# Attention products on 64x64 tiles, one turn of outputs ahead of the transposes, scores two steps ahead

## Chip, core and metric

The kernel runs on one core of a Trainium2 chip. The metric is the device time of one execution in microseconds (us). Where several executions are timed, their median is given.

## What is computed

Two blocks follow each other: an attention with a decaying state (`lightning_attn`) and a mixer with a two-layer product (`mixer_low_rank`).

```python
B, H, S, D = 4, 8, 768, 64          # q, k, v
block = 64
for b in range(S // block):
    intra = einsum('bhic,bhjc->bhij', qb, kb) * Dmask      # lam ** (i - j) for i >= j, else 0
    intra = einsum('bhij,bhjd->bhid', intra, vb)
    inter = einsum('bhid,bhde->bhie', qb * lam_pow, kv_state)
    out[:, :, sl] = intra + inter
    kv_state = lam_block * kv_state + einsum('bhsd,bhse->bhde', kb_dec, vb)
x = out as (B, S, H * D)
h = x.T @ U @ V                      # rank 32
u = x + h.T
result = u + relu(u @ w_ch1) @ w_ch2 # 512 -> 2048 -> 512
```

All of it is fp32. Everything that the change touches lies in the attention and in the first part of the mixer (`x`, `h`, `u`).

## The kernel before

The tokens are cut into 24 tiles of 128 (six for each of the four batches, `NS = 24`, `NT = 6`), and a tile is one step `s`. The kernel works with blocks of 128 tokens where the reference has 64, which gives the same result with other powers of `lam`. The eight heads form four pairs `a` of two heads `x`.

What a step does, by its names in the code:

- `prep` turns `q` and `k` on TensorE (PE): four transposes into the PSUM tile `pq`, four into `pk`. ScalarE (ACT) copies them to `qt` and `kt`, and the next loads of `q` and `k` are issued on SyncE's queue (SP).
- `scale` and `scale_k` multiply on GpSimd (POOL): `qs` is `qt` with the powers for the state's part of the outputs, `ks` is the raw `k` with those for the state's update.
- `scores` are the products of `kt` and `qt` into two PSUM banks, `pss` (token by token, four pairs, two heads). `masked` multiplies them by the decay mask on VectorE (DVE) into `sm`.
- `inter` is the state's part of the outputs, `qs` by `kv[s]`, into two banks `px`. `intra` adds `sm` by `v` to the same sums, and ACT copies the sum to `x_nat`, the tile of `x`.
- `state` is `ks` by `v` into the bank `pkv`; DVE adds to it the faded old state (`faded`, four small ACT instructions made by `fade`) and stores `kv[s+1]`. The load of the next `v` follows.

From the seventh step on, the mixer's first part runs between these: `low` (the rank-32 product of a whole batch, at the first step of the next batch) and `low_rows`, `mix` (one product, and a DVE addition that makes `u` of a tile that lies seven steps back), `turn` (four transposes of `u`, its store to memory as `u_d`, and the split of its values on DVE), and `turned` (the rest of the split on ACT and POOL). `aside` are pieces of the preparation of the weights, on DVE and, late, on ACT.

The instructions run on each engine in the order in which the code calls them (`manual_schedule`). That order is a list written out by hand, `pieces`, made step by step in the loop that the diff shows. Before the change it is, in a step s: transposes of s+1, `mix`, (`low`), outputs of s, state of s, scores of s+1, the state's part of the outputs of s+1, mask of s+1, `turn`.

PSUM has eight banks here: `pss` two, `px` two, and `pq`, `pk`, `pt` and `pu` one each. All have one buffer, so the next writer waits for the last reader. `pkv` shares the bank of `pk`, `mix` writes to `pu`. In SBUF, `qt`, `kt`, `qs`, `ks` and `kv` have two buffers, `sm` and `faded` one, `x` nine, the raw `q` and `v` three and the raw `k` four.

A product on PE runs on a part of its 128x128 array: the profile writes it as rows*columns, `128*64` for 128 contracted rows and 64 columns of weights. An fp32 product shows as two records.

After the last step the first large products start (`pz`, line 731, and `pd`, line 741), with the last tiles' `mix` and `turn` woven in by hand. They and the second ones (lines 864 to 868) fill TensorE to the end.

Of the kernel before, what the change touches and what calls it, by code (L numbers as in the profile page):

```python
# [8 lines left out]
FP32 = mybir.dt.float32  # L9
# [3 lines left out]
ALU = mybir.AluOpType  # L13

P = 128
# [3 lines left out]
def kernel(  # L19
# [28 lines left out]
    nc = tc.nc  # L48
# [203 lines left out]
    def two_banks(name, tag):  # L252
        return psf.tile([P, 2, N], FP32, tag=tag, name=name)
# [2 lines left out]
        return psf.tile(shape, FP32, tag=tag, name=name)  # L256


    psa = []

    def bank(shape, name, tag):
# [9 lines left out]
    def load(name, s, engine):  # L271
        b, c = divmod(s, NT)
        t = raw_pool.tile(
            [P, H, D], FP32, tag=f"{name}raw", bufs=4 if name == "k" else 3, name=f"{name}raw"
        )
        source = {"q": q, "k": k, "v": v}[name]
        n = H if name == "v" else H // parts(s)
        for h in range(0, H, n):
            engine.dma_start(
                out=t[:, h : h + n, :],  # L280
                in_=source[b, h : h + n, c * P : (c + 1) * P, :].rearrange("h p d -> p h d"),
            )
        raw[s, name] = t
# [50 lines left out]
    xs = {}  # L334
# [25 lines left out]
    def prep(s):  # L360
        for a0 in range(0, HP, HP // parts(s)):
            for name in "qk":
                turn_half(s, a0, name)
        st[s].update(qt=qts.pop(s), kt=kts.pop(s))
        for name in "qk":
            load_next(name)

    def scale_k(s):
        st[s] = {}
        if s % NT < NT - 1:  # L370
            st[s]["ks"] = ks = att.tile([P, HP, 2, D], FP32, tag="ks", bufs=2, name="ks")
            nc.gpsimd.tensor_tensor(
                out=ks,
                in0=raw[s, "k"].rearrange("p (a x) d -> p a x d", x=2),
                in1=rev.rearrange("p x a -> p a x").unsqueeze(3).broadcast_to([P, HP, 2, D]),
                op=ALU.mult,
            )

    def scale(s):

        if s % NT > 0:
            st[s]["qs"] = qs = att.tile([P, HP, P], FP32, tag="qs", bufs=2, name="qs")
            nc.gpsimd.tensor_tensor(out=qs, in0=st[s]["qt"], in1=powq, op=ALU.mult)  # L383
        if s + 1 < NS:
            scale_k(s + 1)

    def fade(s):

        if 0 < s % NT < NT - 1:
# [1 line left out]
            for a in range(HP):  # L391
                nc.scalar.mul(faded[:, a, :], kv[s][:, a, :], lamc[:, a, :])

    def scores(s):
        qt, kt = st[s]["qt"], st[s]["kt"]
        st[s]["pss"] = pss = two_banks("pss", "pss").rearrange("p x (a i) -> p x a i", a=HP)
        for a in range(HP):
            for x in range(2):
                for rows in half if s >= 2 * NT else [slice(0, P)]:
                    nc.tensor.matmul(  # L400
                        out=pss[rows, x, a, :], lhsT=kt[half[x], a, rows],
                        rhs=qt[half[x], a, :], start=True, stop=True,
                    )

    def masked(s):
        pss = st[s].pop("pss")
        st[s]["sm"] = sm = att.tile([P, 2, HP, P], FP32, tag="sm", bufs=1, name="sm")
        for x in range(2):
            nc.vector.tensor_tensor(out=sm[:, x], in0=pss[:, x], in1=mask[:, x], op=ALU.mult)  # L409

    def state(s):
        c = s % NT
        if c < NT - 1:
            ks, vr = st[s]["ks"], raw[s, "v"]
            pkv = one_bank([P, HP, D], "pkv", "pk")
            for a in range(HP):
                for x in range(2):
                    nc.tensor.matmul(  # L418
                        out=pkv[half[x], a, :], lhsT=ks[:, a, x, :], rhs=vr[:, 2 * a + x, :],
                        start=True, stop=True,  # L420
                    )
            kv[s + 1] = att.tile([P, HP, D], FP32, tag="kv", bufs=2, name="kv")
            if c == 0:
                nc.vector.tensor_copy(out=kv[s + 1], in_=pkv)
            else:
                nc.vector.tensor_tensor(out=kv[s + 1], in0=pkv, in1=st[s]["faded"], op=ALU.add)
        del st[s]
        del raw[s, "v"]
        load_next("v")

    def inter(s):

        st[s]["px"] = both = two_banks("px", "px")
        px = both[:, :, 0 : HP * D].rearrange("p x (a e) -> p x a e", a=HP)
        if s % NT == 0:
            return

        for a in range(HP):
            for x in range(2):
                for t in range(2):  # L440
                    nc.tensor.matmul(  # L441
                        out=px[half[t], x, a, :], lhsT=st[s]["qs"][half[x], a, half[t]],
                        rhs=kv[s][half[x], a, :], start=(a == 0), stop=False,
                    )

    def intra(s):
        first = s % NT == 0
        sm, vr, px = st[s]["sm"], raw[s, "v"], st[s]["px"]
        px = px[:, :, 0 : HP * D].rearrange("p x (a e) -> p x a e", a=HP)
        for a in range(HP):  # L450
            for x in range(2):
                for t in range(2):
                    nc.tensor.matmul(  # L453
                        out=px[half[t], x, a, :], lhsT=sm[:, x, a, half[t]],
                        rhs=vr[:, 2 * a + x, :], start=(first and a == 0), stop=(a == HP - 1),
                    )
        xs[s] = x_pool.tile([P, C], FP32, tag="x", name="x_nat")
        nc.scalar.copy(xs[s].rearrange("p (a x e) -> p x a e", a=HP, x=2), px)


    pps = {}

    def low(b):

        tag = "pq" if b else "pu"
        pp = one_bank([P, P], "pp", tag) if b < B - 1 else bank([P, P], "pp", "b2")
        for c in range(NT):
            for g in range(G):
                nc.tensor.matmul(  # L469
                    out=pp[g * R : (g + 1) * R, :], lhsT=u_w[:, c, :],  # L470
                    rhs=xs[b * NT + c][:, g * P : (g + 1) * P],
                    start=(c == 0), stop=(c == NT - 1),
                )
        pps[b] = pp
# [33 lines left out]
    def next_of_low(b):  # L508
        pps[b].pop(0)()

    def mix(s):
        b, c = divmod(s, NT)
        pu = one_bank([P, C], "pu", "pu") if s < NS - NT - 1 else bank([P, C], "pu", "b2")
        nc.tensor.matmul(
            out=pu, lhsT=v_hl[:, c * P : (c + 1) * P], rhs=p_hl, start=True, stop=True
        )
        nc.vector.tensor_tensor(out=xs[s], in0=pu, in1=xs[s], op=ALU.add)

    uhl, ud, turned = {}, {}, {}
    hl_at, d_at = [hl_pool], [d_pool]  # L520
# [37 lines left out]

    pieces = [("prep", 0), ("scale", 0), ("scores", 0), ("inter", 0), ("masked", 0)]
    for s in range(NS):
        b, c = divmod(s, NT)
        done = s - NT - 1
        more = s + 1 < NS
        step = [("prep", s + 1), ("scale", s + 1)] * more + [("fade", s)] * (c == 1)
        step += [("late", s - 1)] * (s == NT)
        step += [("mix", done)] * (0 <= done < NS - NT - 1)
        step += [("low", b - 1)] * (c == 0 and b > 0)
        step += [("low_rows", b - 1)] * (c == 0 and b > 0)  # L570
        step += [("intra", s)]
        step += [("next_of_low", b - 1)] * (c == 0 and b > 0)
        step += [("late", s)] * (s < NT - 1 or s == NT) + [("state", s)]
        step += [("next_of_low", b - 1)] * (c == 0 and b > 0)
        step += [("turned", done - 1)] * (done > 0) + [("late", s)] * (done >= 0)
        step += [("next_of_low", b - 1)] * (c == 0 and b > 0)
        step += [("scores", s + 1)] * more
        step += [("aside", s)] * (s >= 2 * NT)
        step += [("inter", s + 1), ("masked", s + 1)] * more
        step += [("fade", s + 1)] * (more and c > 0)  # L580
        step += [("aside", s)] * (s < 2 * NT)
        step += [("turn", done)] * (done >= 0 and done // TG < FG)
        pieces += step
    waiting = {name: list(range(NS)) for name in "qkv"}

    def load_next(name, engine=nc.sync):
        if waiting[name]:
            load(name, waiting[name].pop(0), engine)
# [1 line left out]

    run = {
        "prep": prep, "fade": fade, "scores": scores, "masked": masked, "inter": inter,
        "intra": intra, "state": state,
        "low": low, "low_rows": low_rows, "next_of_low": next_of_low, "mix": mix, "turn": turn,
        "scale": scale, "turned": lambda s: turned.pop(s)(),
    }
# [71 lines left out]
    nc.scalar.dma_start(out=lam_row[:, 0:H], in_=lam.unsqueeze(0))  # L668
    load_next("q", nc.sync)
    load_next("k", nc.scalar)  # L670
    for name in "qkvkv":
        load_next(name)
    aside(-1)
    for name in "qkv":
        load_next(name)
    make_identity(nc, ident)
    keep_busy(2)
    pl = one_bank([P, H], "pl", "pt")
# [3 lines left out]
    constants()  # L682
    powers()
    nc.vector.tensor_copy(out=rev, in_=mask[:, :, :, P - 1])
    scale_k(0)
    run.update(aside=aside, late=on_scalar_late)
    for what, s in pieces:
        run[what](s)
# [278 lines left out]
```

## Time and profile before

| | us |
|---|---|
| median of three runs | 673.26 (672.52 to 673.44) |
| the profiled execution | 672.44 |
| its span, first to last instruction | 670.6 |
| TensorE busy in it | 664.3 |
| DVE, ACT and POOL busy in it | 497.5, 277.8 and 112.1 |
| first `px` product, first `pz` product | 8.87 and 119.65 |

The granted TensorE clock was 1.0 all through. The attention stage, from the start to about 119 us, is less than a fifth of the span and holds nearly all of POOL's work. A busy engine in the profile is one that has an instruction in it: matmuls overlap, and their ends are modelled, so starts are the better measure on PE. A bracket at the end of a line of the timeline tells how long the engine had been idle before it, and what ended that.

### The profile page before, as it was taken

To read this page: it belongs to the slowest core of one execution; us is meant where nothing else is said; L and a number is where in the kernel's file an instruction comes from. 1 tells how busy PE (TensorE), PEld (TensorE's weight loads), DVE (VectorE), ACT (ScalarE), POOL (GpSimd) and SP (SyncE) were. 2 spreads that over 40 slices of the span, in tenths; PEclk is the share of its full clock that TensorE was granted. 3 is DMA by queue.
4 is the path that set the end of the run, shared out by engine and by line. 5 is a ranking of instruction groups with operands and counts; after the bars stand their busy time and mean duration, and the time that the engine had idled before them with its cause. 6 is when DMAs were issued, how large, how long until landed. Compare 5 with 4: busy or idle time off the path is not lost.

```text
span 670.6 us, 13171 instructions
## 1 busy us (share of the span) xinstructions
PE 664.3 (99%) x5124; PEld 544.3 (81%) x5124; DVE 497.5 (74%) x873; ACT 277.8 (41%) x517; POOL 112.1 (17%) x92
## 2 busy tenths in 40 slices
PE   9999999999999999999999999999999999999997
PEld 7988989788888888888888888888888888888885
DVE  5688999877999777777797256787586775865864
ACT  4675867554555444444454121332322322322320
POOL 4555757330000000000000000030030300300300
PEclk9999999999999999999999999999999999999999
DMA  9999993254776555555577999854363352443421
GB/s 208 220 217 244 238 243 114 89 197 157 257 260 235 205 203 205 204 204 205 203 282 270 314 321 394 285 182 132 94 218 96 116 199 94 162 152 95 165 86 63
DMA packets 131775, 131.27 MB, mean 196 GB/s; under 512 B 81346, under 2 KB 89794, under 8 KB 131714
## 3 DMA queue, kind: packets, MB, share of 16 engines
q1 hardware_dynamic: 130656, 130.18, 60.8%
q8 instruction: 40, 0.66, 0.4%
q10 hardware_dynamic: 1058, 0.26, 0.2%
q14 instruction: 21, 0.17, 0.1%
HBM read 80.09 MB, written 50.33 MB: 194 GB/s over the span
## 4 chain that ended last, share of the span: by engine, by line
PE 95%; DVE 2%; DMA 1%; ACT 1%; issue 0%; ACTq 0%; SPq 0%; DVEq 0%
PE pz L731 27%; PE pz L866 13%; PE pd L741 13%; PE pz L864 13%; PE pd L868 13%; PE px L453 3%; PE pss L400 3%; PE put L531 1%; PE pkv L418 1%; PE pq L355 1%; PE px L441 1%; PE pk L355 1%; PE pp L469 1%; DVE sm L409 1%; DMA u_d<-x_nat 1%; DMA kraw<-in_k_dram 1%
## 5 line engine op out<-in xcount | busy, mean ns | idle before, releaser
L731 PE MATMUL pz<-u_hl,w 128*128 128x512 f32 x768 | 190.5, 398 | 0.0
L731 PEld LDWEIGHTS pz<-u_hl,w 128*128 128x128 f32 x768 | 144.1, 189 | 35.3 <-issue 0.4
L866 PE MATMUL pz<-w_hl,m 128*128 128x512 f32 x384 | 151.2, 397 | 0.0
L864 PE MATMUL pz<-w_hl,m 128*128 128x512 f32 x384 | 151.0, 397 | 0.0
L868 PE MATMUL pd<-w_d,m 128*128 128x512 f32 x384 | 149.6, 397 | 0.0
L847 ACT ACTIVATE m<-mt 128x512 fp32r<-128x512 f32 x96 | 60.6, 632 | 196.9 <-PE pd L868 142.3
L848 DVE SCALAR_TENSOR_TENSOR m<-rm,m 128x512 fp32r<-128x512 f32 x96 | 71.4, 746 | 54.5 <-ACT m L847 54.3
L893 POOL TENSOR_TENSOR o<-o,u 128x512 f32<-128x512 f32 x20 | 29.8, 1520 | 447.4 <-DVE o L889 447.4
L746 DVE SCALAR_TENSOR_TENSOR r<-pd,r 128x512 f32<-128x512 f32 x96 | 61.8, 686 | 53.2 <-ACT r L737 38.8
L741 PE MATMUL pd<-u_d,w 128*128 128x512 f32 x384 | 98.6, 397 | 0.0
L737 ACT ACTIVATE r<-pz 128x512 f32<-128x512 f32 x96 | 52.2, 596 | 93.0 <-PE pz L731 92.9
L866 PEld LDWEIGHTS pz<-w_hl,m 128*128 128x128 f32 x384 | 72.4, 189 | 17.6
L864 PEld LDWEIGHTS pz<-w_hl,m 128*128 128x128 f32 x384 | 72.4, 188 | 17.6
L868 PEld LDWEIGHTS pd<-w_d,m 128*128 128x128 f32 x384 | 72.4, 189 | 17.5
L741 PEld LDWEIGHTS pd<-u_d,w 128*128 128x128 f32 x384 | 72.2, 189 | 17.2
L849 DVE SCALAR_TENSOR_TENSOR m<-m 128x512 fp32r<-128x512 f32 x96 | 69.1, 721 | 0.9
L846 DVE TENSOR_SCALAR mt<-rm 128x512 uint32<-128x512 uint32 x96 | 46.1, 481 | 26.5 <-DMA rm<-r_d 26.2
L409 DVE TENSOR_TENSOR sm<-pss,mask 128x512 f32<-128x512 f32 x48 | 30.9, 684 | 6.8 <-PE pss L400 6.6
L212 ACT CAST w<-wt 128x512 fp32r<-128x512 f32 x32 | 19.9, 621 | 30.6 <-DVE wt L209 23.4
L453 PEld LDWEIGHTS px<-vraw,sm 128*64 128x64 f32 x768 | 24.6, 138 | 5.9 <-DVE sm L409 2.3
L383 POOL TENSOR_TENSOR qs<-qt,powq 128x512 f32<-128x512 f32 x20 | 25.9, 1296 | 20.7 <-ACT qt L358 20.7
L453 PE MATMUL px<-vraw,sm 128*64 128x64 f32 x768 | 28.2, 226 | 0.4 <-DVE sm L409 0.3
(88 smaller groups left out, 680.4 us busy)
## 6 DMA issues: line engine op xcount, KB each, us to landing
r_d<-r SPq DMA_DIRECT2D x96, 256.0 KB, 2.6
rm<-r_d SPq DMA_DIRECT2D x96, 256.0 KB, 2.7
words<-in_moe_w_ch_dram SPq DMA_DIRECT2D x30, 512.0 KB, 4.3
w_d<-w SPq DMA_DIRECT2D x16, 768.0 KB, 3.3
w_hl<-w_d SPq DMA_DIRECT2D x16, 512.0 KB, 6.0
vraw<-in_v_dram SPq DMA_DIRECT2D x24, 256.0 KB, 4.8
u_d<-x_nat SPq DMA_DIRECT2D x24, 256.0 KB, 3.6
u<-u_d SPq DMA_DIRECT2D x24, 256.0 KB, 3.9
```

The lines of the kernel that those rows point to most:

```text
L453: nc.tensor.matmul(out=px[half[t], x, a, :], lhsT=sm[:, x, a, half[t]], rhs=vr[:, 2 * a + x, :], start=(first and a == 0), stop=(a == HP - 1),
L731: nc.tensor.matmul(out=acc[g][0], lhsT=w[:, n, ct, :], rhs=uhl[g][:, n, ct, :], start=(ct == 0 and n == 0), stop=(ct == CT - 1 and n == 1),)
L737: nc.scalar.mul(rs[g], acc[g][0], 4096.0 + 1.0)
L741: nc.tensor.matmul(out=acc[g][1], lhsT=w[:, 2, ct, :], rhs=ud[g][:, ct, :], start=(ct == 0), stop=(ct == CT - 1),)
L746: nc.vector.scalar_tensor_tensor(rs[g], acc[g][1], 4096.0, rs[g], ALU.mult, ALU.add)
L846: nc.vector.tensor_scalar(t.bitcast(U32), r.bitcast(U32), HI, None, ALU.bitwise_and)
L847: nc.scalar.activation(out=m[:, 0], in_=t, func=AF.Relu)
L848: nc.vector.scalar_tensor_tensor(m[:, 1], r, 0.0, hi, ALU.max, ALU.subtract)
L849: nc.vector.scalar_tensor_tensor(m[:, 2], hi, E, low, ALU.mult, ALU.subtract)
L864: nc.tensor.matmul(out=pz, lhsT=m[:, 0, cols], rhs=hl[:, 0], start=first, stop=False)
L866: nc.tensor.matmul(out=pz, lhsT=m[:, 1, cols], rhs=hl[:, 1], start=False, stop=end)
L868: nc.tensor.matmul(out=pd, lhsT=m[:, 2, cols], rhs=dd, start=first, stop=end)
```

## The change

- Outputs and state are made in two turns, each of products of 64 tokens (`outputs(s, turn)`). The part of an output that the mask makes zero (late keys, early queries) is left out. In a turn, heads of one parity take the first half of the keys and the others the second, so that two row halves of the array never write one bank together. Turn 0 (`ahead`) stands at the end of step s-1, before the next transposes; turn 1 in `intra`. The last two steps use full columns (`whole`).
- The state's products share the two banks of `px` (`pkv` is a part of it), and `state` is merged into `intra`: the copy to `x_nat` comes first, then `kv`.
- Transposes and scores are made two steps ahead instead of one: a short step -1 is put in front. `pss` becomes one fixed tile, `sm` gets two buffers, the raw `k` three instead of four, with its load in a piece of its own after `scale`.
- `scores` use 64x64 tiles in every step (before, from step 12), and from the second tile on leave out the masked quarter. In steps 0 to 6, where there is no `mix`, the first pair's scores (`some_scores`) stand before `intra` and the others after.
- `fade` stands after `prep`, `turn` at the next step after the transposes, and `mix` is parted: its product stays (now in the bank of `pq`), its addition `mixed` comes after `intra`. `low` of the first three batches uses `pu`.

```diff
@@ load @@
-            [P, H, D], FP32, tag=f"{name}raw", bufs=4 if name == "k" else 3, name=f"{name}raw"
+            [P, H, D], FP32, tag=f"{name}raw", bufs=3, name=f"{name}raw"
...
@@ scale @@
+        scale_k(s)
         if s % NT > 0:
...
-        if s + 1 < NS:
-            scale_k(s + 1)
...
@@ scores @@
+    def scores(s, pairs=range(HP)):
         qt, kt = st[s]["qt"], st[s]["kt"]
-        for a in range(HP):
+        for a in pairs:
             for x in range(2):
-                for rows in half if s >= 2 * NT else [slice(0, P)]:
+                for rows in half:
+                    cols = slice(rows.start if s else 0, P)
                     nc.tensor.matmul(
-                        out=pss[rows, x, a, :], lhsT=kt[half[x], a, rows],
-                        rhs=qt[half[x], a, :], start=True, stop=True,
+                        out=pss[rows, x, a, cols], lhsT=kt[half[x], a, rows],
+                        rhs=qt[half[x], a, cols], start=True, stop=True,
                     )
+    def some_scores(s):
+        scores(s, range(1))
+
+    def other_scores(s):
+        scores(s, range(1, HP))
...
@@ inter @@
+        both = two_banks("px", "px")
+        st[s]["px"] = px = both[:, :, 0 : HP * D].rearrange("p x (a e) -> p x a e", a=HP)
+        st[s]["pkv"] = both[:, :, HP * D : (HP + 2) * D].rearrange("p g (a e) -> p g a e", a=2)
...
+    def outputs(s, turn):
...
+        for a in range(HP):
+            for r in range(2):
+                x = r ^ turn
+                for t in range(r, 2):
+                    nc.tensor.matmul(
+                        out=px[half[t], x, a, :], lhsT=sm[half[r], x, a, half[t]],
+                        rhs=vr[half[r], 2 * a + x, :], start=(x, t) not in begun,
+                        stop=last and a == HP - 1 and (turn == 1 or (x, t) == (0, 0)),
+                    )
+                    begun.add((x, t))
+        if last:
+            return
+        ks = st[s]["ks"]
+        for n in range(2):
+            for r in range(2):
+                side = r ^ turn
+                a = 2 * side + n
+                for x in range(2):
+                    nc.tensor.matmul(
+                        out=pkv[half[x], side, n, :], lhsT=ks[half[r], a, x, :],
+                        rhs=vr[half[r], 2 * a + x, :], start=(side, x) not in begun,
+                        stop=(turn == 1 and n == 1),
+                    )
+                    begun.add((side, x))
...
+    def ahead(s):
+        if s < NS - 2:
+            outputs(s, 0)
+
+    def intra(s):
+        if s < NS - 2:
+            outputs(s, 1)
+        else:
+            whole(s)
         xs[s] = x_pool.tile([P, C], FP32, tag="x", name="x_nat")
-        nc.scalar.copy(xs[s].rearrange("p (a x e) -> p x a e", a=HP, x=2), px)
+        nc.scalar.copy(xs[s].rearrange("p (a x e) -> p x a e", a=HP, x=2), st[s]["px"])
+        if s % NT < NT - 1:
+            kv[s + 1] = att.tile([P, HP, D], FP32, tag="kv", bufs=2, name="kv")
+            to, pkv = kv[s + 1].rearrange("p (g a) d -> p g a d", g=2), st[s]["pkv"]
...
+                nc.vector.tensor_tensor(out=to, in0=pkv, in1=faded, op=ALU.add)
+        del st[s]
+        del raw[s, "v"]
+        load_next("v")
...
@@ mix @@
-        pu = one_bank([P, C], "pu", "pu") if s < NS - NT - 1 else bank([P, C], "pu", "b2")
+        pu = one_bank([P, C], "pu", "pq") if s < NS - NT - 1 else bank([P, C], "pu", "b2")
...
@@ the order @@
-    pieces = [("prep", 0), ("scale", 0), ("scores", 0), ("inter", 0), ("masked", 0)]
-    for s in range(NS):
+    pieces = [("prep", 0), ("scale", 0), ("scores", 0), ("masked", 0)]
+    for s in range(-1, NS):
...
-        step = [("prep", s + 1), ("scale", s + 1)] * more + [("fade", s)] * (c == 1)
+        step = [("prep", s + 2), ("scale", s + 2), ("load_k", s)] * more
+        step += [("fade", s)] * (s >= 0)
         step += [("late", s - 1)] * (s == NT)
-        step += [("mix", done)] * (0 <= done < NS - NT - 1)
-        step += [("low", b - 1)] * (c == 0 and b > 0)
-        step += [("low_rows", b - 1)] * (c == 0 and b > 0)
-        step += [("intra", s)]
...
-        step += [("late", s)] * (s < NT - 1 or s == NT) + [("state", s)]
+        step += [("turn", done - 1)] * (done > 0 and (done - 1) // TG < FG)
+        mixes = 0 <= done < NS - NT - 1
+        step += [("mix", done)] * mixes
+        step += [("low", b - 1), ("low_rows", b - 1)] * batch
+        apart = s >= 0 and more and not mixes
+        step += [("some_scores", s + 2)] * apart
+        step += [("intra", s)] * (s >= 0)
+        step += [("mixed", done)] * mixes
...
-        step += [("scores", s + 1)] * more
-        step += [("aside", s)] * (s >= 2 * NT)
-        step += [("inter", s + 1), ("masked", s + 1)] * more
-        step += [("fade", s + 1)] * (more and c > 0)
-        step += [("aside", s)] * (s < 2 * NT)
-        step += [("turn", done)] * (done >= 0 and done // TG < FG)
+        if s < 0:
+            step += [("inter", 0), ("ahead", 0), ("scores", 1), ("masked", 1)]
+        else:
+            step += [("other_scores" if apart else "scores", s + 2)] * more
+            step += [("aside", s)] * (s >= 2 * NT)
+            step += [("inter", s + 1), ("ahead", s + 1)] * next_
+            step += [("masked", s + 2)] * more
+            step += [("aside", s)] * (s < 2 * NT)
```

## The prediction

> **What bounds the kernel now.** I read the page first, then busy time by stage, then the waits and the timeline of the attention stage.
>
> ```profile
> PE   9999999999999999999999999999999999999997
> PE 95%; DVE 2%; DMA 1%; ACT 1%; issue 0%; ACTq 0%; SPq 0%; DVEq 0%
> ...
> 7.00:28.00 21.00, 20.90 (x490) 18.72 (x486) 11.01 (x25) 13.02 (x34) 11.55 (x10) 1.00 0.99 226
> 66.00:95.75 29.75, 29.41 (x756) 26.55 (x754) 28.34 (x50) 20.65 (x46) 20.16 (x16) 1.00 0.96 238
> ```
>
> The first two lines are the page's PE row of 40 slices and the chain that ended last: TensorE from end to end. The last two are stretches (length, busy PE, weight loads, DVE, ACT, POOL, clock, DMA share, GB/s). Even with DMA 99% busy, PE has no holes, and in the second stretch DVE is nearly full too (28.34 of 29.75). All that changes lies before 119.65 us, where the last `px` product gives way to `pz`; what follows is one unbroken PE stream, so time won or lost here moves the end by as much. The waits of that stage give PE almost none: 2.3 us over nine times on `sm`, 0.7 on `x_nat`, 0.3 on `kt`.
>
> Why there are none is seen in one early step, then in a step with the mixer's pieces (start, duration, engine, what):
>
> ```profile
> 16.74 0.66 PE L355 MATMUL pq<-ident,qraw 128*128 128x128 f32 x4
> ...
> 17.49 0.59 ACT L358 COPY qt<-pq 128x512 f32<-128x512 f32 x1 [0.70 <-PE pq L355]
> ...
> 17.76 1.15 PE L453 MATMUL px<-vraw,sm 128*64 128x64 f32 x32
> ...
> 17.97 0.59 ACT L358 COPY kt<-pk 128x512 f32<-128x512 f32 x1
> ...
> 18.75 0.64 PE L418 MATMUL pkv<-vraw,ks 128*64 128x64 f32 x16
> 18.96 0.59 ACT L458 COPY x_nat<-px 128x512 f32<-128x512 f32 x1 [0.40 <-PE px L453]
> ...
> 19.31 1.16 PE L400 MATMUL pss<-qt,kt 64*128 64x128 f32 x16
> ...
> 19.50 0.42 DVE L426 TENSOR_TENSOR kv<-pkv,faded 128x256 f32<-128x256 f32 x1 [1.25 <-PE pkv L418]
> ...
> 20.40 0.72 PE L441 MATMUL px<-kv,qs 64*64 64x64 f32 x32
> ...
> 21.05 0.66 PE L355 MATMUL pq<-ident,qraw 128*128 128x128 f32 x4
> ```
>
> ```profile
> 100.41 1.15 PE L453 MATMUL px<-vraw,sm 128*64 128x64 f32 x32
> ...
> 101.01 1.07 ACT L392 ACTIVATE faded<-kv,powq 128x64 f32<-128x64 f32 x4
> ...
> 101.40 0.64 PE L418 MATMUL pkv<-vraw,ks 128*64 128x64 f32 x16
> ...
> 101.96 1.10 PE L400 MATMUL pss<-qt,kt 64*64 64x128 f32 x32
> ...
> 102.89 0.64 PE L441 MATMUL px<-kv,qs 64*64 64x64 f32 x32
> ...
> 103.46 0.66 PE L531 MATMUL put<-ident,x_nat 128*128 128x128 f32 x4
> ```
>
> The copy of `kt` (until 18.56) lies beside `px`. `x_nat` (until 19.55) lies beside `pkv` and `pss`. `kv` (until 19.92) lies beside `pss`, and the product that needs it starts at 20.40, 0.48 later. An early step is 4.31 us (16.74 to 21.05), a mixer step 4.74 (95.67 to 100.41).
>
> **What the skill says.** (1) "TensorEngine Tiling (Array Packing)", Key Properties: changing the tiling mode drains TensorE. The trace agrees: single starts are 0.15 us apart from the last `pkv` record to the first `pss`, 0.05 inside a group. (2) "TensorE: Matmul & The Clock Gate", Part 3: matmuls on different tiles of the array run together, about 4 ns apart. The trace has 7 ns. On one tile, records follow each other every 0.058 us with 64 columns (in `px`, `pkv` and the 64x64 `kv` product alike) and 0.109 with 128. Each fp32 product is two records. So a group's price is the records on its fullest tile times these. (3) "PSUM — Partial Sum Buffer", bank collisions: two engines must not use one bank and quadrant at once, reads included. No run here shows a collision; the wait built from it is below.
>
> **The change, part by part.**
>
> *Products.* `px` before: 32 records on two tiles, 16 x 0.058 = 0.93 (0.98 seen). After: 24 records per turn on three of four tiles, 8 on the fullest, 0.46 per turn, 0.93 for both. `pkv` before 8 x 0.058 = 0.47, after 4 per turn, 0.23 each: the same. `pss`: the 64-column pieces lie on other tiles than the 128-column ones, so 8 x 0.109 = 0.87 stays (0.93 seen), except that steps before 12 had 1.09. Masking half the outputs saves work, not time on the fullest tile. What goes is one change of mode per step, 0.15, and in early steps 0.2 of `pss`.
>
> *Where the outputs stand.* Turn 0 moves to the end of the step before. Between the transposes and the scores there is now 0.70 instead of 1.45 of products, and in steps 0 to 6 a quarter of the scores stands before even that: it waits for `kt`, which ends 1.82 after the first transpose (18.56 - 16.74), while the eight transposes leave PE at 1.02. That is a wait of 0.85, with everything on PE queued behind it.
>
> *`pkv` moves into `px`'s banks.* Both are now one tile, so in the changed program's order `x_nat` waits for the last state product, and `kv` on DVE waits for ACT's `x_nat` copy. The `kv` product waits for `kv`. Before, `x_nat` and `kv` ran side by side. Now it is a chain after turn 1: 0.27 from PE's last start to ACT (18.69 to 18.96), 0.58 copy, 0.03, 0.42 for `kv`, 0.05: 1.35 us. Its cover is 0.87 of scores in mixer steps, 0.65 in early ones. Behind the waiting product stand turn 0 and all transposes of the next step.
>
> *`fade` moves.* Its four ACT instructions (1.07) now stand between the copy of `kt` and `x_nat`, where before they followed `kv`; ACT runs in order. So `x_nat` cannot start before T+2.82, T being the first `q` transpose: 0.75 to `qt` (17.49 - 16.74), 0.48 to `kt`, 0.59, 1.00 (faded to the next ACT start).
>
> *The rest.* `mix` now writes `pq`'s bank and waits for `qt`: 0.16, hidden in the ACT chain. `ks` waits for turn 1 (two buffers, one step further ahead), and POOL then has 1.06 + 1.28 + 1.28 = 3.6 us per step: it fits. On SP, the load of `k` (one buffer less) waits for that `ks`, and the load of `v`, the store of `u_d` and the weight words queue behind it; each tile is needed over 10 us later and lands in about 5, so nothing. Not so the store: `x` has nine buffers, so `x_nat` of step s waits until the `u_d` store of tile s-9 has landed. That store is now issued in step s-1, behind the load of `k`: turn 1's last start 2.50, `ks` to 3.83, two issues of 0.5, so T+4.4. A store lands 2.2 to 5.5 after its issue (median 3.8, view of the tile `u_d`), so at T+8.2, where `x_nat` could start at T+5.22+2.82 = T+8.04. I take 0.16 for the eight steps 9 to 16 where DMA is crowded, 1.3 in all; the ends are 0 and 0.8 in each of 12 steps, 9 us. Early loads land every 0.9 us (6.2, 7.0, 7.95 in the trace); `k3`, now thirteenth, lands near 15.2 for a use at 16.9. DVE has about 4.5 us of work per mixer step (28.34 us over 6.3 steps): it fits a period of 5.2 but not one much below 4.7. `turn` comes a step later, which removes the 0.7 wait on `x_nat`.
>
> *Sum.* From the end of `kv` to the next T: 0.05 + 0.05 (first start after a wait) + 0.46 + 0.64 + 0.17 (change of mode) = 1.37. Mixer step with fade (states 1 to 4): 2.82 + 0.58 + 0.03 + 0.42 + 1.37 = 5.22. Early step: scores start 1.87, quarter 0.27, last start of turn 1 at 2.81, `x_nat` 3.08 to 3.66, `kv` to 4.11, T' = 5.48. Last step of a batch (no `kv`, no fade): 4.34 early, 4.0 later. First step with `low` (1.45): 6.3 at step 6, 6.75 at 12 and 18. Start of step 0: scores(0) end 7.65, mask to 9.14, turn 0, scores(1): 11.0. Then 11.0 + 5 x 5.48 + 4.34 + 6.3 = 49.0; steps 7 to 10, 20.9; 11, 4.0; 12, 6.75; 13 to 16, 20.9; 17, 4.0; 18, 6.75; 19 to 21, 15.7; 22 (no scores as cover: 2.4 to the last start, 1.3 chain, 0.7), 4.4; 23, 2.0. The sum is 134.4, against 119.65: +14.8, with the stores +16.1. The profiled execution took 672.44 around a span of 670.6: 688.5. The median of three is 0.8 higher, 673.26, so I say 689.
>
> **Unknown costs.** Three tiles in a turn are not seen in this trace. Lower end: as four tiles (0.46 a turn). Upper end: the two records of a product don't interleave well and a turn takes 0.23 more; that is 0.46 per early step and some 0.4 per mixer step, +9. I take the lower end, since two and four tiles both interleave. Waits could be off by 0.1 each at three places in 21 steps: 6 either way. Heavy weight pieces on DVE may delay `kv`: up to 1.5. The forecast's own range is 682 to 697.
>
> **Rivals.** A (faster): PE's own work decides, because the engines' chains stay covered as before. Then a mixer step is 4.53 (4.74 less 0.15 and the switch's slow second start, 0.05) and an early one 3.9. It gives 12 x 0.2 + 7 x 0.35, about 5 us less: 668. For it: ACT is 60 to 70% busy, and nothing but the order of its work hurts. Against it: it needs the chain after turn 1 to fit 0.87, and it counts 1.35. It decides if that chain is under 0.9. B: only the early steps lose, since mixer steps have `put` and `mix` before turn 1: 6 x 1.15 = 7 less 2 of switches, 678. Against it: `fade` holds `x_nat` to T+2.82 there too. C: poor packing on three tiles on top of the forecast: 698. It needs turns of 0.93 where the trace's 64x64 group takes 0.57 for more records.
>
> **Chances.** Forecast 0.70, A 0.09, B 0.08, C 0.13. 0.2% of the time is about what a measurement tells from none. B at its low edge holds the chance of no change. Range 677 to 698: it holds the forecast's, B and half of C.
>
> **What would show it.** Right: PE idle 0.7 to 0.9 before `pss` in steps 0 to 6 until ACT `kt`; PE idle 0.5 to 0.7 before the `kv` product until DVE `kv`; DVE idle before `kv` until ACT `x_nat`; steps of 5.2 to 5.5; `pz` starting near 134. Wrong: steps under 4.7, `kv` ending before the scores do, or turns taking 0.7 for `px` alone.

## The result, and the profile after

The changed kernel takes 698.00 us (median of four runs, 694.83 to 699.12) against 672.89 for the kernel before in the same comparison: a ratio of 1.0365 (95% interval 1.0346 to 1.0385). The forecast said slower, 689 in a range of 677 to 698. The direction and most of the steps hold. The time is 9 us above the sum: it lies at the upper edge of that range, and outside the 682 to 697 that the forecast gave to its own sum.

The profiled execution took 698.99 around a span of 697.2. The first `pz` product starts at 146.40, where it started at 119.65: +26.75, which is the whole difference of the spans (26.6). Everything behind that point is unchanged. The page shows where TensorE has holes now, and how the chain that ended last is made up:

```profile
PE   8788989899999999999999999999999999999997
...
q8 instruction: 47, 0.77, 0.5%
...
PE 84%; issue 4%; DVE 2%; POOL 1%; ACT 0%; DMA 0%; DVEq 0%
```

The PE row has a 7 and 8s in the first eight slices (before, 9s). In the chain PE falls from 95% to 84%, and `issue` rises from 0 to 4%: time in which an engine waited for nothing that the profile shows. The `q8` line counts the transfers by which instructions are fetched: 47, before 40.

The view of the waits up to 150 us names the forecast's chain (who waited for whom, total, times, longest):

```profile
DVE kv L501 <- ACT x_nat L493: 24.3, 14, 5.8
...
PE px L425 <- POOL ks L371: 5.5, 12, 0.6
...
PE pss L397 <- ACT kt L359: 4.6, 6, 0.8
...
PE px L454 <- issue: 3.6, 4, 1.3
...
PE px L425 <- DVE kv L501: 3.4, 6, 1.5
...
PE pk L356 <- DMA kraw<-in_k_dram: 1.2, 1, 1.2
```

`kv` (L501) waits for the copy to `x_nat` (L493), the product that needs `kv` (L425) waits on TensorE, and the early scores (L397) wait for `kt`. For some of the L425 waits the profile names POOL's `ks`, which happens to end nearby; but in 19 of 20 steps the product starts 0.15 us after the end of `kv`, wherever `ks` ends. One early step, and the matching lines of a mixer step (start, duration, engine, what, idle time before it):

```profile
29.47 0.66 PE L356 MATMUL pq<-ident,qraw 128*128 128x128 f32 x4
...
30.70 0.59 ACT L359 COPY kt<-pk 128x512 f32<-128x512 f32 x1
...
31.34 0.43 PE L397 MATMUL pss<-qt,kt 64*64 64x128 f32 x7 [0.78 <-ACT kt L359]
...
32.56 0.58 ACT L493 COPY x_nat<-px 128x512 f32<-128x512 f32 x1 [0.31 <-PE px L454]
...
33.17 0.42 DVE L501 TENSOR_TENSOR kv<-px,faded 128x256 f32<-128x256 f32 x1 [3.22 <-ACT x_nat L493]
...
33.74 0.69 PE L425 MATMUL px<-kv,qs 64*64 64x64 f32 x32 [0.62 <-POOL ks L371]
...
35.07 0.33 PE L356 MATMUL pq<-ident,qraw 128*128 128x128 f32 x1
```

```profile
94.46 0.66 PE L356 MATMUL pq<-ident,qraw 128*128 128x128 f32 x4
...
97.28 0.59 ACT L493 COPY x_nat<-px 128x512 f32<-128x512 f32 x1
...
97.90 0.42 DVE L501 TENSOR_TENSOR kv<-px,faded 128x256 f32<-128x256 f32 x1 [0.45 <-ACT x_nat L493]
...
98.47 0.69 PE L425 MATMUL px<-kv,qs 64*64 64x64 f32 x32 [0.40 <-POOL ks L371]
...
99.80 0.65 PE L356 MATMUL pq<-ident,qraw 128*128 128x128 f32 x4
```

An early step is 5.60 us (29.47 to 35.07) and a mixer step 5.34 (94.46 to 99.80), in the order that the forecast wrote down: `kt` lets the scores go, turn 1, `x_nat`, then `kv`, then TensorE.

What the forecast did not have is in the steps that are longer than that. Steps 1, 8, 9 and 13 take 7.83, 7.39, 6.79 and 7.31, and steps 12 and 18, the first of a batch, 7.38 and 8.23 where 6.75 was forecast. Around the boundary of steps 8 and 9:

```profile
61.93 0.43 PE L454 MATMUL px<-vraw,ks 64*64 64x64 f32 x14
...
63.69 0.21 PE L454 MATMUL px<-vraw,ks 64*64 64x64 f32 x1 [1.33 <-issue]
...
63.83 0.96 PE L356 MATMUL pq<-ident,qraw 128*128 128x128 f32 x4
...
64.58 1.06 PE L356 MATMUL pk<-ident,kraw 128*128 128x128 f32 x4
```

Two things are seen here. TensorE stops for 1.33 us in the middle of a group of state products, with one of them left, and the profile names no releaser (nothing whose end released it). Then the transposes, 0.60 to 0.66 in other steps, take 0.96 and 1.06: the granted clock was 0.5 from 64.04 to 67.45. It was also 0.5 from 19.67 to 23.08, after the 1.17 us wait for `k3` and the 0.73 for `kt`.

The gaps named `issue` can be explained from the trace's records of the instruction queue, which hold each 16 KB transfer. All gaps without a releaser of over 0.3 us in the attention stage:

```
gap ends at   length   last q8 transfer ended   between
   59.13       0.31          57.69               1.44
   63.69       1.33          62.21               1.47
   84.33       0.38          82.85               1.48
   94.15       1.25          92.74               1.40
  119.02       0.56         117.60               1.42
  122.92       0.35         121.45               1.47
  137.46       0.65         135.93               1.53
```

Every one ends 1.40 to 1.53 us after a transfer of q8 ended. (One more, 0.34 before the first `mix` product at 52.53, does not, and is left out.) The number of transfers grows with TensorE's work: the changed kernel has 424 more products, which are 1,696 records with their weight loads, and 7 more transfers, so one for some 240 records. I read the gaps as TensorE out of instructions. No record shows the queue empty; runs 7 to 9 below test the reading.

Added up from the trace, TensorE's idle time is 4.6 us before the early scores, 9.7 before the state's part of the outputs, 1.2 for `k3` and 4.8 out of instructions, and half clock costs some 3.4 (an estimate: two stretches of 3.41 at half speed). That is 23.7 of the 26.75. Idle time understates the two waits, because it is counted from the modelled end of a product. Counted from the start of the last product to the start of the next, the pauses before the state's part of the outputs make 15.1 in 20 steps, against 2.9 in the kernel before, and the six before the early scores 6.3, where the kernel before goes on after 0.20 each, 1.2. With these differences, 12.2 and 5.1, the same sum is 26.7.

### The profile page after: what moved, and what is told of

It reads as the page before. It is cut to its first block, busy times and chain, and to the rows that moved or that the text cites. A ratio compares the mean times of both kernels' runs of the same rounds, so it can differ in the third digit from the quotient of the medians.

```text
span 697.2 us, 14831 instructions
## 1 busy us (share of the span) xinstructions
PE 671.1 (96%) x5972; PEld 545.7 (78%) x5972; DVE 501.2 (72%) x873; ACT 278.1 (40%) x517; POOL 112.2 (16%) x92
## 4 chain that ended last, share of the span: by engine, by line
PE 84%; issue 4%; DVE 2%; POOL 1%; ACT 0%; DMA 0%; DVEq 0%
PE pz L790 26%; PE pz L925 13%; PE pz L923 13%; PE pd L800 13%; PE pd L927 13%; PE px L440 1%; PE px L425 1%; PE put L583 1%; POOL ks L371 1%; PE pq L356 1%; PE px L454 1%; PE pk L356 1%; PE pu L561 1%; DVE sm L411 0%; ACT x_nat L493 0%
## 5 line engine op out<-in xcount | busy, mean ns | idle before, releaser
L397 PE MATMUL pss<-qt,kt 64*64 64x128 f32 (+1 forms) x768 | 29.4, 256 | 4.7 <-ACT kt L359 4.6
L440 PE MATMUL px<-vraw,sm 64*64 64x64 f32 x1056 | 32.1, 224 | 0.8 <-issue 0.7
L359 ACT COPY qt<-pq 128x512 f32<-128x512 f32 (+1 forms) x25 | 14.2, 569 | 44.2 <-PE pq L356 44.1
```

The source lines that it names most:

```text
L440: nc.tensor.matmul(out=px[half[t], x, a, :], lhsT=sm[half[r], x, a, half[t]], rhs=vr[half[r], 2 * a + x, :], start=(x, t) not in begun, st ...
```

## The experiments

**1. The state's bank.** The state's products go back to a bank of their own, as full columns after turn 1:

```diff
+        st[s]["pkv"] = pkv = one_bank([P, HP, D], "pkv", "pk")
+        for a in range(HP):
+            for x in range(2):
+                nc.tensor.matmul(
+                    out=pkv[half[x], a, :], lhsT=ks[:, a, x, :], rhs=vr[:, 2 * a + x, :],
+                    start=True, stop=True,
+                )
```

> Changed kernel with the state's products back in a bank of their own (that of pk), as one group of full columns after turn 1. Theory (the copy to x_nat and then kv, one after the other on one bank pair, make TensorE wait before the state's part of the outputs): these waits, 9.65 us in all in the changed kernel's trace (0.62 in early steps, 0.40 in mixer steps), fall to under 1.5 in steps up to 21, while two more changes of tiling mode at 0.15 in some 20 steps cost 6. Net -2, and with 8 products fewer per step some of the 4.8 us of waits for instructions go as well: 693 (690 to 697). Rival (the chain is not what TensorE waits for, only the order of the work): the waits before that product stay, and the modes' 6 us come on top: 704.

Measured: 686.83 (686.38 to 687.16), 1.0189 of before (1.0167 to 1.0211), 11 us less than the changed kernel. A mixer step in the timeline of TensorE alone:

```profile
90.78 0.60 PE L572 MATMUL put<-ident,x_nat 128*128 128x128 f32 x4
...
91.67 0.69 PE L439 MATMUL px<-vraw,sm 64*64 64x64 f32 x24
92.28 0.69 PE L466 MATMUL pkv<-vraw,ks 128*64 128x64 f32 x16
92.90 0.99 PE L397 MATMUL pss<-qt,kt 64*64 64x128 f32 x30
...
93.77 0.63 PE L424 MATMUL px<-kv,qs 64*64 64x64 f32 x28
...
95.77 0.60 PE L572 MATMUL put<-ident,x_nat 128*128 128x128 f32 x4
```

No bracket is left: nothing is waited for, and the step is 5.00. The waits before the state's part of the outputs fall from 9.7 to 2.1 (1.4 of it in the last such step); the theory's chain is what TensorE waited for. `pz` starts 13.3 us earlier than in the changed kernel's profile, which is one of its slower executions. From start to start, the pause before the state's part falls from 15.1 to 3.9, more than the 8 that were expected from idle time. Besides, no stretch has half clock (some 3.4), the gaps out of instructions are 2.3 instead of 4.8, and the wait for `k3` is 0.9 shorter. These make 18.1. The 4.8 that are missing from the gain are near the 6 that were expected for two more changes of mode: each shows as 0.15 between two starts, where in the changed kernel outputs, state and scores follow each other at mostly 0.05 or less.

**2. The part alone, in the kernel before.** Only the state's place is changed, with `x_nat` copied after it:

```diff
-            pkv = one_bank([P, HP, D], "pkv", "pk")
+            pkv = st[s]["pkv"]
...
+        xs[s] = x_pool.tile([P, C], FP32, tag="x", name="x_nat")
+        nc.scalar.copy(xs[s].rearrange("p (a x e) -> p x a e", a=HP, x=2), px)
```

> Kernel before with one part of the change: the state's products go to the free part of px's banks, and the copy to x_nat comes after them, then kv. Everything else, order and tiles, stays. Theory: the chain after the last state product (0.27 to ACT, 0.58 copy, 0.42 kv, 0.13 back to TensorE = 1.4) ends 0.25 to 0.3 after the scores in early steps and 0.4 to 0.45 after them in mixer steps, so TensorE waits before the state's part of the outputs; 5 x 0.27 + 13 x 0.43 = 7, 680 to 681. Rival (the scores cover the chain): no change, 673.

Measured: 683.65 (682.67 to 685.73), ratio 1.0140 (1.0108 to 1.0173). In a mixer step of it:

```profile
115.59 1.10 PE L400 MATMUL pss<-qt,kt 64*64 64x128 f32 x32
...
115.70 0.58 ACT L414 COPY x_nat<-px 128x512 f32<-128x512 f32 x1 [1.10 <-PE px L423]
...
116.32 0.42 DVE L435 TENSOR_TENSOR kv<-px,faded 128x256 f32<-128x256 f32 x1 [0.96 <-ACT x_nat L414]
...
116.89 0.69 PE L451 MATMUL px<-kv,qs 64*64 64x64 f32 x32 [0.20 <-POOL ks L372]
```

The product stands 1.30 behind the scores' start; in the kernel before it is 0.93. From step 13 on, mixer steps are 5.17 instead of 4.73 (+0.44, expected +0.43), and early steps 4.50 instead of 4.30 (+0.20, expected +0.27). The rival, that the scores cover the chain, is out. From start to start, the pauses before the state's part make 13.1 us in 20 steps, against 2.9 in the kernel before. That difference, 10.1, is nearly the whole shift of `pz`, 10.2 (from 119.65 to 129.90). The total is 3 us above the sum, but by other terms. Steps 6, 12 and 18, the first of a batch, are 1.5 to 2.1 longer, 5.2 together, because `x_nat` stands behind two more copies of `low` on ACT (0.62 each); in the kernel before and in the changed one it stands ahead of them. And steps 7 to 10 bring only 0.4 in all, because the kernel before takes 4.95 to 5.38 for them.

**3. `k3` earlier.** Its load is issued ahead of that of the fifth `q`:

```diff
-    pieces = [("prep", 0), ("scale", 0), ("scores", 0), ("masked", 0)]
+    pieces = [("prep", 0), ("scale", 0), ("load_k", 0), ("scores", 0), ("masked", 0)]
```

> Changed kernel with only the load of the fourth k tile moved ahead, so that it is issued before the loads of the fourth and fifth q. Theory (the wait of 1.2 us for that tile also brings the half clock of 3.4 us that follows it): step 1 goes from 7.83 to about 5.6 us, no half clock near 20 us, total 695.8. Rival (the half clock comes whatever the wait): step 1 about 6.6, total 696.8. Third (a later tile is late instead): no change, 698.

In the trace the load still stands behind that of the fourth `q`, not ahead of it as expected; it is issued at 11.44 instead of 13.50 and lands at 15.98 instead of 17.82.

Measured: 696.57 (695.41 to 700.29), which the total can't tell from 698.00. The trace can: the wait for `k3` is gone, step 1 takes 5.60, and no stretch before `pz` has half clock. `pz` starts 2.6 earlier, at 143.84. That agrees with half clock following the pause, but is one profile: by their mean clocks of 0.999, two of the changed kernel's own four runs have no such stretches either.

**4 and 5. The wait for `kt`, and `fade`.** In steps 0 to 6 all scores stand behind turn 1, and one product of a single column, waiting for `qt`, stands where the first pair's were. The second run has `fade` behind `kv` as well:

```diff
-        apart = s >= 0 and more and not mixes
+        apart = False
...
+        nc.tensor.matmul(out=out, lhsT=ident, rhs=st[s]["qt"][:, 0, 0:1], start=True, stop=True)
```

> Changed kernel in which the steps 0 to 6 no longer put the first pair's scores ahead of turn 1; in their place stands one product of a single column that waits for the copy of qt. Theory: the wait of 0.78 for kt shrinks to about 0.35, but x_nat cannot start before the fade ends, 2.8 after the first transpose, where it starts at 3.1 now: -0.3 in each of 5 steps, -1.5, 696.5. Rival (the wait for kt is the whole price of the early steps): -0.8 in each of 6 steps, 693.

> The same as the run with the single column product, and the fade moved behind kv as in the kernel before. Theory (fade is what holds x_nat once the wait for kt is gone): x_nat 2.5 after the first transpose, early steps 5.0 instead of 5.6, mixer steps as they were (fade holds x_nat by 0.03 there): -3, 695. Rival (fade does not matter): as the run with the single column product alone, 696.5.

Measured: 696.34 (695.41 to 697.94) and 695.93 (695.40 to 697.17). The wait before turn 1 falls from 0.78 to 0.29, and the one before the state's part from 0.62 to 0.40. Step 4, which no other gap disturbs, takes 4.98 and 4.97 against 5.37. In it `x_nat` starts 2.70 after the first transpose in the first run, directly behind `fade`, and 2.69 in the second, where it waits for turn 1. So `fade` in its old place brings nothing, and the rival to the second expectation holds. In the totals both are within the spread of the changed kernel's runs: `issue` gaps (5.2 us over seven in the trace of the second run) take back what the steps give.

**6. Scores on 64x64 tiles, alone, in the kernel before:**

```diff
-                for rows in half if s >= 2 * NT else [slice(0, P)]:
+                for rows in half:
```

> Kernel before with one part of the change: scores on 64x64 tiles in the early steps too. TensorE's own time: a change of mode less in 11 steps, 0.16 each in the trace of before (1.09 from the scores to the next product against 0.92): -1.8, 671 to 672. Rival from the instructions' side: 8 products more per step bring waits for instructions, and the gain is eaten: 673 or more.

Measured: 676.84 (15 runs, 674.56 to 679.17), ratio 1.0035 (1.0016 to 1.0054): slower by 2 to 3 us. The early steps do get shorter, 4.07 to 4.20 instead of 4.3. What is late next is a store:

```profile
52.90 0.58 ACT L458 COPY x_nat<-px 128x512 f32<-128x512 f32 x1 [2.50 <-DMA u_d<-x_nat]
...
53.59 0.63 PE L441 MATMUL px<-kv,qs 64*64 64x64 f32 x27 [0.93 <-ACT x_nat L458]
```

The copy to `x_nat` waits for its buffer until the `u_d` store of an earlier tile has landed, 9.1 us over five times (1.3 once in the kernel before). Neither expectation had this. Only 1.0 us of `issue` on TensorE stands beside it, so the instructions are not the main cause; why the store weighs as much as it does there was not separated from a late `q` load (0.8) near 13 us.

**7 to 9. Instructions.** Products of one column are added to the kernel before, their sums unread: 16 on full rows behind the state's products, then 16 and 32 on the four 64x64 tiles behind the state's part of the outputs:

```diff
+        for i in range(32):
+            r, c = i % 2, i // 2 % 2
+            nc.tensor.matmul(
+                out=both[half[c], r, HP * D + i : HP * D + i + 1], lhsT=ident[half[r], half[c]],
+                rhs=ident[half[r], 0:1], start=False, stop=False,
+            )
```

> Kernel before with 16 products of a single column added behind the state's products of each of 20 steps, their results unread, on full rows and the same tile size as those; 85 products in a mixer step as in the changed kernel. Their own time on TensorE is 16 records per tile at no more than 0.058: up to 0.93 a step, 6 to 19 in all, 679 to 692. Theory (TensorE outruns the supply of its instructions when products become more and smaller): gaps appear in which TensorE waits for nothing, at least 4 of over 0.25 us in the attention stage, each ending 1.2 to 1.55 us after a transfer of the instruction queue ended. Rival (the gaps of the changed kernel belong to its order or to its 64x64 turns): none appears, as in the kernel before.

> Kernel before with 16 products of a single column added behind the state's part of the outputs, on 64x64 tiles, their sums unread; they go to all four tiles, so PE starts a record every 15 ns where the 128x64 ones of the earlier run start one every 29. Own time 8 records per tile x 0.058 = 0.46 a step in 20 steps: +9, 682. Theory (not the number of products decides but how fast a stretch uses them up: the four tile groups outrun the transfers of the instruction queue): gaps in which TensorE waits for nothing appear, 2 or more of over 0.25 us, each ending 1.2 to 1.55 us after such a transfer. Rival (gaps come from the changed kernel's waits or order): none.

> The same with 32 products: +0.93 a step, 18.6 in all, 691. Theory: more of these gaps than with 16, at least 5 and 3 us in all. Rival: none.

Measured: 688.42 (688.27 to 690.91), 683.67 (680.63 to 686.71, two runs) and 706.57 (703.84 to 709.31, two runs). The first has not one gap of over 0.15 us in the stage after its first products, though it has the changed kernel's number of products per mixer step. The second has two of over 0.2, of 2.05 and 1.14, ending 1.40 and 1.45 after a transfer. Its profile is that of the slower run; the faster one, 680.63, is not above the 682 expected for the products' own time, so the gaps may not come in every execution. The third has 15 of over 0.2, 11.4 us in all, 1.25 to 1.57 after one; it makes 50 transfers. Two lines of it:

```profile
112.07 0.71 PE L447 MATMUL px<-ident 64*64 64x1 f32 x40
114.20 0.53 PE L447 MATMUL px<-ident 64*64 64x1 f32 x24 [1.42 <-issue]
```

A group of equal products that depend on nothing stops in its middle. So gaps came into the kernel before, without the change's waits, with products on four tiles, and not with the same number on two: this points to the rate at which a stretch uses instructions up, not to their sum (the two groups also stand at different places of the step and write other banks, which no run separates). The rival of runs 8 and 9, that no gap appears, is out, and the theory of run 7, that their number makes the gaps, fell with that run.

**10. All repairs at once:** runs 1, 3 and 5 together.

> Changed kernel with all the repairs at once: state in a bank of its own, the single column product in place of the early scores, fade behind kv, the fourth k earlier. Theory: early steps 4.7 (5.16 with the bank alone, less the 0.5 of the wait for kt), mixer steps stay at 5.0, which is TensorE's own time with nothing waited for; 683 to 684, so still slower than the kernel before. Rival (waits alone made the change slow): 670 or less.

Measured: 685.95 (684.95 to 687.16), ratio 1.0171 (1.0140 to 1.0203). Early steps are 4.88 to 4.95 and mixer steps 5.00, so with the chain's waits gone this kernel still loses to 4.3 and 4.73. It does not beat run 1 by more than the spread: TensorE's waits for `qt` before `mix`, which shares its bank, have come in their place (2.4 us in two steps). The time is far from the rival's 670, but that does not put the rival, that waits alone made the change slow, out: like run 1, this kernel has two changes of mode per step more than the changed one, and 8.5 us of idle time on TensorE are left in its stage. At 0.15 each, the two changes are up to 0.3 of the 5.00. So the changed kernel's mixer step without waits is 4.7 or somewhat more, as an estimate, about the 4.73 of the kernel before. No run shows a changed kernel with neither the waits nor those changes of mode.

## Why the prediction was right, and where it was short

- **What bounds.** Right. All of the loss lies before `pz`, and the stream behind it moved as a block. One reading was off without harm: the 2.3 us on `sm`, 0.7 on `x_nat` and 0.3 on `kt` in the kernel before are waits of weight loads; the products themselves wait 0.3, 0.4 and 0.2.
- **Products.** Right in size: a turn takes 0.69 (`0.46` and `0.23` were forecast), so three tiles pack as well as four. Rival C's cause did not occur; that its 698 is the measured time is chance. Since the range reaches above 697 only for rival C, it is luck, too, that the time still lies in it.
- **The wait for `kt`.** Forecast 0.85, measured 0.78.
- **`pkv` in `px`'s banks.** Right, and shown by taking it out (run 1) and putting it in alone (run 2). The early step was forecast at 5.48 and is 5.60, the mixer step 5.22 and 5.33, mostly because DVE to TensorE took 0.15 where 0.05 was written. The last steps of a batch (4.34 and 4.0) are 4.33, 4.06 and 4.27.
- **`fade`.** In the forecast it holds `x_nat` to T+2.82. `x_nat` does start at T+2.82 in a mixer step, but turn 1 ends there too: with `fade` moved back (run 5) mixer steps stay at 5.33. So the number was right, and `fade` was not what set it alone.
- **The stores.** The 1.3 us did not come: no wait of TensorE in the changed kernel is for a `u_d` store. The mechanism is real, as run 6 shows, where the early steps are faster; that the slower steps of the changed kernel are what spared it is not shown.
- **The loads.** This step failed. "`k3`, now thirteenth, lands near 15.2 for a use at 16.9": it was issued at 13.50, behind two `q` loads, and landed at 17.82. The order was known, but the landing was taken from a run of loads with no waits between. It cost 1.17 us, and half clock came after it.
- **What the sum had no term for.** The sum from waits was +16.1 and the result +26.75. Instructions that come too late are 4.8 of the missing 10.6, half clock 3.4, `k3` 1.2. "Waits could be off by 0.1 each" came true with some 1.5, which the missing stores balance; about 1 us of the difference stays open. The forecast counted records per tile and never how many instructions a stretch holds.
- **Rival A.** The chain after turn 1 didn't fit under the scores, so its condition failed. The 4.53 that it gave TensorE's own work in a mixer step seems too low as well: the estimate from run 1 is 4.7. Leaving out the masked part saved nothing on the fullest tile, as the forecast said: from first to last start the scores take 0.82 in a mixer step, before 0.84.

## What to carry to other kernels

Two results that share a bank, kept as one tile, were read one after the other here: moving a state sum into its neighbour's bank turned two copies side by side into a chain, at 0.20 us in an early step and 0.44 in a late one. When products are made smaller and spread over all tiles, count instructions per microsecond as well as records per tile (runs 7 to 9 point to it), and look for `issue` gaps in the middle of uniform groups. A step that gets shorter early meets the next limit, here a buffer that is held by a store, so a local gain is not yet a gain.

## What the runs showed of the hardware

- In the gaps of the changed kernel and of runs 8 and 9, TensorE resumed 1.25 to 1.57 us after the end of an instruction transfer; the transfers themselves took 0.9 to 1.9. Why one transfer comes late and the next in time stays open.
- Half clock came in stretches of 3.41 us, and the times at which the clock changed lie multiples of that apart (23.08 and 64.04 in the changed kernel: 40.96, or twelve). Cut at these times into stretches of 3.41 (where there is no half clock, from the start of the clock's first record), TensorE was idle for 1.9 and 1.7 us in the ones before the changed kernel's half clock, and for 2.05 in run 8. Those with 1.45 to 1.53 idle, one in each of six kernels, were followed by full clock, and so was a pause of 1.78 in run 2 that lay across a border (1.03 and 0.75). Run 9 had half clock after 0.9 to 1.2 idle, between products of one column, and not after 1.3, so idle time alone is not the measure. The changed kernel's four runs had mean clocks of 0.994, 0.999, 0.995 and 0.999 at 699.0, 697.0, 699.1 and 694.8 us, so by these means the stretches don't come in every execution.
